# The last two blocks' down projection by two levels of a seven-product scheme instead of one

## Chip, cores and metric

The kernel runs on one core of a Trainium2 chip. The metric is the device time of one execution in microseconds (us). Times of the kernel before are the median of three runs; the profile is one further execution.

## The reference, cut to what matters

```python
kv  = np.einsum('bhsd,bhse->bhde', k, v)          # 8 batches, 8 heads, 576 positions, 64 wide
o   = np.einsum('bhsd,bhde->bhse', q, kv)
o   = o / np.sqrt(np.mean(o * o, -1, keepdims=True) + 1e-6) * g_norm
x   = o.transpose(0, 2, 1, 3).reshape(4608, 512)
g   = x @ w_gate                                  # 512 -> 1536
out = (g / (1 + np.exp(-g)) * (x @ w_val)) @ w_out   # 1536 -> 512, fp32
```

## The kernel before

The 4608 tokens are cut into nine blocks of 512 (0 to 8). Each block is taken through attention, then through the gate and value products ("up", 512 to 1536), then through w_out ("down", 1536 to 512). Matrix products are made by a scheme of seven block products for a 2 by 2 cut (a Strassen-like one, in the order 1, 5, 6, 2, 7, 4, 3 or a variant). Products 1, 6, 7, 4 accumulate one after another in one PSUM tile called b, 5 and 3 in one called c, and 2 in one called a; between two of them the partial sum is read out by ScalarE (copy) or VectorE (add). The scheme needs sums of blocks of both operands: side sums of h (the hidden activations), and differences of w_out's blocks.

Blocks 0, 1 and 2 go alone. From block 3 on, blocks go in pairs (class `Pair`): 3 and 4, 5 and 6, 7 and 8. In a pair's up stage both blocks are multiplied together and by two levels of the scheme, seven outer times seven inner products. For this, class `Inner` walks six pairs of feature columns, j = 0 to 5; each j has four groups of outer products, and each group makes its seven inner products. The weights' leaves for it lie in DRAM and stream through SBUF tiles `t` (nine buffers, class `Stream`, loads on SP's queue; a load is put in program order where the tile that it will replace is used for the last time). During group 2's products GpSimd makes four small additions (`made1`), after group 3 a 1024-wide one (`made2`), and after group 4 two 1024-wide multiplications (`made3`), which give h; then the side sums of block a's h. For j = 5 VectorE does the multiplications instead. All these results live in five ring buffers `r`.

The down stage (class `Down`, `multiply` in line 661's helper) is different: it takes one block after the other, and by one level. Each of a block's seven products is 12 matmuls: two output halves times six steps of 128 contracted features, 128 stationary columns and 256 moving ones. The moving operand is w_out (`wo`) or a difference of its quarters that GpSimd makes into `t` tiles (`turn_t`), so the results come out in rows of tokens and are stored as they are by SP's queue (`store`, line 1122). For the last block, the third product is made in two halves in PSUM tiles m (line 1032), the second of them as the very last work. The side sums of the second block of a pair (`second_sums`) are made by GpSimd during the first block's down stage. TensorE's order in a down stage is fixed as the program has it.

Line 816 is an inner product of the up stage, line 661 a product of the single-level stages, line 431 the attention's product with q, line 494 a transposition on TensorE. Lines 130, 131 and 132 are the helpers for additions, subtractions and multiplications; line 522 sends transposed pieces of x from SBUF to SBUF, 16 transfers of 64 KB on the queues of SP and ScalarE.

Of the kernel before, what the change touches and what calls it, by code (L numbers as in the profile page):

```python
# [8 lines left out]
F32 = mybir.dt.float32  # L9
# [9 lines left out]
def kernel(  # L19
# [84 lines left out]
    kvs = [consts.tile([P, NS, D], F32, name=f"kv{i}") for i in range(3)]  # L104
# [29 lines left out]
    @contextmanager  # L134
    def in_order(*engines):

        traced = nc.cur_bb.bb.instructions
        last = traced[-1]
        yield
        start = next(k for k in reversed(range(len(traced))) if traced[k] is last) + 1  # L140
        before = {}
        for i in traced[start:]:
            if engines and i.engine not in engines:
                continue
            if i.engine in before:
                tc.add_manual_dep(
                    i, before[i.engine].name,
                    mybir.DependencyInfo(mybir.DependencyClass.NoSync, mybir.DependencyReason.DATA), reason="order",
                )
            before[i.engine] = i  # L150

# [488 lines left out]
    class Quad:  # L640


        def __init__(self, steps):
            self.steps = steps
            self.ps, self.room = {}, None

            self.apart = {}

# [3 lines left out]
        def multiply(self, p):  # L652
            name, first = CHAIN[p]
            if first:
                tiles = [PSUMS[name].tile([P, 2, HB], F32, name=name) for _ in range(1 + (name in self.apart))]
                self.ps[name], self.apart[name] = tiles[0], tiles[-1]
            banks = self.ps[name], self.apart[name]
            for e, i in self.order(p):
                lhsT, rhs = self.operands(p, e, i)

                self.ffn.multiplied = nc.tensor.matmul(  # L661
                    banks[e][:, e], lhsT=lhsT, rhs=rhs, start=first and i == 0 and (e == 0 or banks[0] is not banks[1]),
                    stop=i == self.steps - 1, skip_group_check=True,
                )
            getattr(self, f"after{p}", lambda: None)()
# [91 lines left out]
    class Inner:  # L757
# [94 lines left out]
        def made3(self, p, e, q):  # L852
            if p != 4:
                return
            h = h_both[:, :, 2 * self.j : 2 * self.j + 2]
            halves = lambda t: t.rearrange("p (b e) t -> p b e t", b=2)
            c11, c12, c21, c22 = (self.whole(*i) for i in ((1, 1), (3, 1), (3, 0), (1, 0)))

            engine = nc.gpsimd if self.j + 1 < NP else nc.vector
            mul(engine, h[:, :, :, 0:HB], halves(c11), halves(c12))  # L860
            with tc.issue_after(self.ffn.fifth.ins):
                nc.scalar.activation(out=c21, in_=c21, func=ACT.Silu)
            mul(engine, h[:, :, :, HB:BLK], halves(c21), halves(c22))
            self.ffn.ended = self.ffn.a.h_sums(self.j, 1, engine)

# [13 lines left out]
    class Stream:  # L879
# [15 lines left out]
        def pump(self):  # L895

            while self.next and not self.held[-9]:
                n, j, c = key = self.next.pop(0)
                tile_ = t_tile(key)
                os, ps = JOINT[c]  # L900
                count = len(os) * len(ps)
                self.tiles[key] = tile_.rearrange("p a (b c) -> p (a b) c", c=P)
                self.uses[key] = count
                to = self.tiles[key][:, 0:count].rearrange("p (o i) c -> p o (i c)", o=len(os))
                src = self.dram[:, j, steps_of(OUTERS, os), steps_of(INNERS, ps)].rearrange("p o i c -> p o (i c)")
                nc.sync.dma_start(out=to, in_=src)

        def use(self, n, j, o, p):
            c, i = self.joint[o, p]
            key = n, j, c  # L910
            self.uses[key] -= 1
            if not self.uses[key]:
                self.free(key)
            return self.tiles[key][:, i]
# [4 lines left out]
    stream = Stream()  # L919
# [65 lines left out]
    class Down(Quad):  # L985
        def __init__(self, ffn):
            super().__init__(NP)
            self.ffn = ffn
            self.t = {}
            self.final = ffn.n == NB - 1  # L990
            self.lone = False
            self.opens = None
            self.keeps = False
            if self.final:
                self.apart["c"] = None
# [16 lines left out]
        def multiply(self, p, es=(0, 1)):  # L1012
            if p == 3 and self.lone:
                self.third(es)
                return
# [7 lines left out]
        def third(self, es):  # L1023


            if es[0] == 0:
                tiles = [m_psum.tile([P, 2, HB], F32, name="m") for _ in range(1 + self.final)]
                self.thirds = tiles[0], tiles[-1]
            for e in es:
                for i in range(self.steps):  # L1030
                    lhsT, rhs = self.operands(3, e, i)
                    self.ffn.multiplied = nc.tensor.matmul(  # L1032
                        self.thirds[e][:, e], lhsT=lhsT, rhs=rhs, start=i == 0 and (e == 0 or self.final),
                        stop=i == self.steps - 1, skip_group_check=True,
                    )
            if not self.final:
                add(nc.vector, self.o1[:, :, HD:DM], self.thirds[0], self.u2)
                self.ffn.store(self.o1, 0)
                return
            for e in es:  # L1040
                add(nc.vector, self.o1[:, e, HD:DM], self.thirds[e][:, e], self.u2[:, e])
                self.ffn.store(self.o1[:, e : e + 1, HD:DM], e, slice(HD, DM))

        def after6(self):
            super().after6()
            if self.lone:
                self.add_c(self.u2, self.u2)

        def order(self, p):
            order = [(e, i) for e in range(2) for i in range(self.steps)]  # L1050
            return order if p == 3 and self.final else sorted(order, key=lambda ei: ei[1])
# [17 lines left out]
        def rows(self):  # L1069
            o = ring()  # L1070
            self.o1, self.o2 = o[:, 0:2], o[:, 2:4]

        def after2(self):
            if self.lone:
                self.rows()
            add(nc.vector, self.o1[:, :, 0:HD], self.ps["a"], self.s)
            if self.final:
                self.ffn.store(self.o1[:, :, 0:HD], 0, slice(0, HD))
# [4 lines left out]
        def after7(self):  # L1083
            if not self.lone:
                self.rows()
            u3 = self.piece(2)
            nc.scalar.copy(out=u3, in_=self.ps["b"])
            self.add_c(self.o2[:, :, HD:DM], u3)
# [5 lines left out]
        def after3(self):  # L1094
            self.add_c(self.o1[:, :, HD:DM], self.u2)
            if not self.final:
                self.ffn.store(self.o1, 0)
                return
            for e in range(2):
                self.ffn.store(self.o1[:, e : e + 1, HD:DM], e, slice(HD, DM))  # L1100

        def add_c(self, o, u):

            if not self.final:
                add(nc.vector, o, self.ps["c"], u)
                return
            for e, c in enumerate((self.ps["c"], self.apart["c"])):
                add(nc.vector, o[:, e], c[:, e], u[:, e])

    class Ffn:  # L1110
# [9 lines left out]
        def store(self, o, t, columns=slice(None)):  # L1120
            rows = out[BLK * self.n : BLK * (self.n + 1), columns].rearrange("(t p) d -> p t d", t=T)
# [40 lines left out]
        def down(self, nxt, then={}):  # L1162
# [3 lines left out]
            down.lone = nxt is None  # L1166
            order = (1, 6, 5, 7, 2, 4, 3) if 5 in fill else (1, 5, 6, 7, 2, 4, 3)
            if down.lone:
                order = (1, 5, 6, 2, 7, 3, 4)
            for p in order:  # L1170
# [5 lines left out]
                with tc.issue_after(nxt.multiplied.ins) if self.n == 0 and p in (5, 6) else ExitStack():  # L1176
                    down.multiply(p, *[(0,)] * (p == 3 and down.lone and down.final))
# [14 lines left out]
            if down.lone and down.final:  # L1192
                down.multiply(3, (1,))
# [25 lines left out]
    class Pair:  # L1219


        def __init__(self, n):
            self.n = n
            self.a, self.b = (Ffn(i, blocks[i]) for i in (n, n + 1))
            self.visited = None

        def up(self, fill):

            a = self.a
            a.s1 = s_pool.tile([P, NP, HB], F32, name="s1")  # L1230
# [5 lines left out]
            for i, this in enumerate(units):  # L1236
                for unit, p in this.sequence(last):
                    if unit:
                        visited, self.visited = self.visited, None
                        with tc.issue_after(visited.ins) if visited else ExitStack():  # L1240
                            unit.multiply(p)
                last = this
                fill.get(i + 1, lambda: None)()
            a.down_ = Down(a)
            a.down_.keeps = True
            a.down_.turn_t(5)
# [3 lines left out]
            a.ended = self.ended  # L1250
# [165 lines left out]
    for n in range(PAIRED, NB, 2):  # L1416
# [3 lines left out]
        if after:  # L1420
# [10 lines left out]
            for i in range(8):  # L1431
                fill[12 + i] = lambda i=i, after=after: after[i // 4].load_quarters(i % 4 // 2, (i % 2,))
        pair.up(fill)
        if after:
            after[0].turn()
        if len(after) > 2:
            after[2].load_kv(0)
        with in_order(nc.tensor.engine):
            pair.a.down(after[0] if after else None, {5: pair.second_sums})
            if after:  # L1440
                after[1].turn()
            if len(after) > 2:
                after[2].load_kv(1)
            pair.b.down(after[1] if after else None)
# [31 lines left out]
```

## Time and profile before

| | |
|---|---|
| median of 3 runs | 1011.48 us (1011.41 to 1013.13) |
| profiled execution | 1012.7 us |
| its span, first to last instruction | 1010.9 us |
| TensorE busy | 993.7 us, 98% |
| VectorE, GpSimd, ScalarE busy | 673.7, 369.6, 232.2 us |
| granted TensorE clock | full (1.000) |
| up stage of blocks 7 and 8 | 806.1 to 934.85 us |
| down stage of block 7, then 8 | 934.85 to 1007.4 us |

PE in the profile is TensorE's matmul side, PEld its weight loads (which run beside the matmuls), DVE is VectorE, ACT is ScalarE, POOL is GpSimd and SP is SyncE, which here only issues DMAs. A line of a timeline has the start, the length, the engine, the line of the code, the operation, the tiles that it writes and reads, the shape and the count; what stands in brackets is the idle time before it and what ended it. An fp32 matmul of the code shows as two records. Every time after a start is counted in us from the first instruction.

### The profile page before, as it was taken

To read this page: it belongs to the slowest core of one execution; us is meant where nothing else is said; L and a number is where in the kernel's file an instruction comes from. 1 tells how busy PE (TensorE), PEld (TensorE's weight loads), DVE (VectorE), ACT (ScalarE), POOL (GpSimd) and SP (SyncE) were. 2 spreads that over 40 slices of the span, in tenths; PEclk is the share of its full clock that TensorE was granted. 3 is DMA by queue.
4 is the path that set the end of the run, shared out by engine and by line. 5 is a ranking of instruction groups with operands and counts; after the bars stand their busy time and mean duration, and the time that the engine had idled before them with its cause. 6 is when DMAs were issued, how large, how long until landed. Compare 5 with 4: busy or idle time off the path is not lost.

```text
span 1010.9 us, 17078 instructions
## 1 busy us (share of the span) xinstructions
PE 993.7 (98%) x6506; PEld 831.6 (82%) x6506; DVE 673.7 (67%) x1121; ACT 232.2 (23%) x367; POOL 369.6 (37%) x290
## 2 busy tenths in 40 slices
PE   5999999999999999999999999999999999999998
PEld 4544688888888888888888888888888888888887
DVE  2999797589868477656676746666668566666311
ACT  2665111221122311212211121121112121121000
POOL 0000263255544240445456004455660026546600
PEclk9999999999999999999999999999999999999999
DMA  8688653483866855767742464667221654553011
GB/s 220 198 266 260 120 93 136 97 288 97 210 136 122 214 114 158 189 179 182 170 130 42 111 164 135 182 164 191 77 42 43 146 164 144 150 145 101 1 42 42
DMA packets 254290, 143.23 MB, mean 142 GB/s; under 512 B 149504, under 2 KB 236544, under 8 KB 254208
## 3 DMA queue, kind: packets, MB, share of 16 engines
q1 hardware_dynamic: 223488, 138.20, 50.8%
q10 hardware_dynamic: 30656, 3.94, 2.5%
q8 instruction: 52, 0.85, 0.4%
q14 instruction: 30, 0.25, 0.1%
q0 software_dynamic: 64, 0.00, 0.0%
HBM read 104.99 MB, written 28.70 MB: 132 GB/s over the span
## 4 chain that ended last, share of the span: by engine, by line
PE 75%; DMA 1%; POOL 0%; SPq 0%; issue 0%; DVE 0%; POOLq 0%
PE b L816 22%; PE b L661 20%; PE c L816 11%; PE c L661 9%; PE a L816 5%; PE a L661 5%; PE m L431 1%; PE m L1032 1%; PE m L370 1%; DMA ld<-in_v_dram 1%; POOL t L131 0%; SPq L312 0%; PE b L370 0%; PE b L431 0%; PE a L431 0%
## 5 line engine op out<-in xcount | busy, mean ns | idle before, releaser
L816 PE MATMUL b<-arena,t 128*128 128x256 f32 x1008 | 244.5, 381 | 0.0
L816 PEld LDWEIGHTS b<-arena,t 128*128 128x128 f32 x1008 | 190.1, 190 | 29.6 <-DVE r L130 2.4
L130 POOL TENSOR_TENSOR r<-r 128x256 f32<-128x256 f32 (+1 forms) x90 | 94.7, 1054 | 246.1 <-DVE r L130 154.9
L130 DVE TENSOR_TENSOR r<-b,r 128x512 f32<-128x512 f32 (+1 forms) x234 | 138.9, 606 | 60.1 <-PE b L816 54.8
L130 DVE TENSOR_TENSOR r<-c,r 128x512 f32<-128x512 f32 (+1 forms) x170 | 104.5, 623 | 81.9 <-PE c L816 40.1
L132 POOL TENSOR_TENSOR arena<-r 128x1024 f32<-128x1024 f32 (+1 forms) x54 | 102.1, 1904 | 112.3 <-DVE r L130 67.9
L131 POOL TENSOR_TENSOR t<-wo 128x512 f32<-128x512 f32 x54 | 76.9, 1445 | 167.8 <-DVE wo L130 105.9
L130 DVE TENSOR_TENSOR r<-a,r 128x512 f32<-128x512 f32 x93 | 59.2, 636 | 108.3 <-PE a L661 70.7
L816 PE MATMUL c<-arena,t 128*128 128x256 f32 x504 | 122.5, 379 | 0.0
L131 DVE TENSOR_TENSOR arena<-arena 128x512 f32<-128x512 f32 (+3 forms) x96 | 104.3, 1101 | 20.0 <-PE b L661 17.7
L816 PEld LDWEIGHTS c<-arena,t 128*128 128x128 f32 x504 | 95.6, 190 | 13.5 <-issue 0.3
L661 PE MATMUL b<-wo,arena 128*128 128x256 f32 x432 | 98.1, 382 | 0.2
L661 PE MATMUL b<-t,arena 128*128 128x256 f32 x432 | 96.2, 379 | 0.0
L661 PEld LDWEIGHTS b<-wo,arena 128*128 128x128 f32 x432 | 81.2, 190 | 12.5 <-DVE arena L132 0.9
L661 PEld LDWEIGHTS b<-t,arena 128*128 128x128 f32 x432 | 82.1, 190 | 11.2
L830 ACT COPY r<-b 128x512 f32<-128x512 f32 x54 | 31.7, 586 | 189.9 <-PE b L816 189.9
L131 POOL TENSOR_TENSOR t<-arena 128x512 f32<-128x512 f32 x36 | 51.1, 1432 | 56.2 <-PE c L661 21.9
L816 PE MATMUL a<-arena,t 128*128 128x256 f32 x252 | 66.1, 379 | 0.0
L816 PEld LDWEIGHTS a<-arena,t 128*128 128x128 f32 x252 | 47.9, 190 | 6.5
L661 PE MATMUL c<-t,s 128*128 128x256 f32 x216 | 48.1, 379 | 0.0
L661 PE MATMUL a<-wo,arena 128*128 128x256 f32 x216 | 48.1, 379 | 0.0
L661 PEld LDWEIGHTS a<-wo,arena 128*128 128x128 f32 x216 | 41.0, 190 | 5.6
(115 smaller groups left out, 1242.9 us busy)
## 6 DMA issues: line engine op xcount, KB each, us to landing
t<-w SPq DMA_DIRECT2D x180, 256.0 KB, 3.1
out_dram<-r SPq DMA_DIRECT2D x17, 512.0 KB, 2.9
ld<-in_k_dram SPq DMA_DIRECT2D x26, 288.0 KB, 4.6
ld<-in_v_dram SPq DMA_DIRECT2D x26, 288.0 KB, 6.1
t<-w SPq DMA_DIRECT2D x54, 128.0 KB, 2.3
ld<-in_moe_w_gate_dram SPq DMA_DIRECT2D x12, 512.0 KB, 4.6
ld<-in_moe_w_val_dram SPq DMA_DIRECT2D x12, 512.0 KB, 4.7
ld<-in_moe_w_out_dram SPq DMA_DIRECT2D x12, 512.0 KB, 4.8
```

The costliest lines, as they stand in the source:

```text
L130: add = lambda e, o, a, b: e.tensor_tensor(out=o, in0=a, in1=b, op=OP.add)
L131: sub = lambda e, o, a, b: e.tensor_tensor(out=o, in0=a, in1=b, op=OP.subtract)
L132: mul = lambda e, o, a, b: e.tensor_tensor(out=o, in0=a, in1=b, op=OP.mult)
L370: self.positions = nc.tensor.matmul(self.kv_ps[r][u * D : (u + 1) * D, g, :], lhsT=k[:, u, c, :], rhs=v[:, u, c, :], start=(c == 0), stop= ...
L431: self.multiplied = nc.tensor.matmul(self.ps[i][u][p : p + D, t, j, :], lhsT=self.qt[rows, tile_t, head, p : p + D], rhs=kvs[b % 3][rows, ...
L661: self.ffn.multiplied = nc.tensor.matmul(banks[e][:, e], lhsT=lhsT, rhs=rhs, start=first and i == 0 and (e == 0 or banks[0] is not banks[1 ...
L816: self.ffn.multiplied = nc.tensor.matmul(ps[:, i], lhsT=stream.use(self.ffn.n, self.j, o, p), rhs=self.operand(o, p), start=first and i == ...
L830: copied = nc.scalar.copy(out=dst, in_=ps)
L1032: self.ffn.multiplied = nc.tensor.matmul(self.thirds[e][:, e], lhsT=lhsT, rhs=rhs, start=i == 0 and (e == 0 or self.final), stop=i == self ...
```

## The change

Blocks 7 and 8 no longer go through `Down`. Classes `Last` and `Deep` take both together and by two levels: seven outer products (grouped (1, 2), (6, 5), (7), (4, 3)) of seven inner ones of three contraction steps. Now w_out's block is the stationary operand and h the moving one: 128 tokens of each of the two blocks, 256 columns. So the results come out turned (features on partitions). Two of the four quarters of the output are transposed by VectorE in blocks of 32 by 32 and sent in 16 transfers of 32 KB each, with pieces of 128 bytes (`send`). The other two come from the last group: three of its four pieces are transposed back by TensorE (`turn_back`). The fourth is the last inner product (number 4 of the last group). Its addend is put into PSUM by four matmuls with the identity, and the product itself is made on top of it with h stationary and w_out moving, so in rows of tokens, as 12 matmuls of 128 columns (`turn_onto`).

The outer and inner side sums of h are made by VectorE in `down` (`outer`, `sum_x`). The weights' inner sums are made by GpSimd in the up stage of blocks 7 and 8: `prepare` lists them, and `tick`, called after every inner product, puts one at a time behind GpSimd's latest instruction at fixed places of a turn (`FIRST`, `TURNS`). First come six operations on wo in place, then nine times a leaf block (one 512-wide, one 128-wide and one 256-wide operation) whose results are written to DRAM by two transfers on SP's queue six ticks later, and twelve differences kept in SBUF. The side sums of h are now made for both blocks at once, 512 wide, twelve ticks after the multiplications, and for every second j four more operations turn them (`turn`). The leaves of outer products 5, 7 and 4 come back as 21 loads behind the last stream loads. The order of TensorE and VectorE in the new stage is that of the program. The kv tiles become one tile with three parts. Code that served only the last block's old form is dropped. Blocks 0 to 6 keep their code path.

```diff
+        def turned_block(self, i, c):
...
+            def send():
+                with behind(nc.sync.engine):
+                    nc.sync.dma_start(out=to[:, 0:5], in_=t)
+                    nc.sync.dma_start(out=to[:, 5:7], in_=more)
+
+            def differences():
+                sub(nc.gpsimd, t[:, 4], t[:, 0], t[:, 1])
+                sub(nc.gpsimd, more, t[:, 2:4], t[:, 1:2].to_broadcast([P, 2, P]))
+                self.sends.append((self.count + 6, send))
...
+        FIRST = {0: (0, 1, 3), 1: (0, 2, 4), 2: (1, 4), 3: (0, 2, 4, 5)}
+        TURNS = {0: (0, 1), 1: (), 2: (4,), 3: (0, 2, 4, 5)}
+
+        def tick(self):
+            g, e = divmod(self.count % 28, 7)
+            self.count += 1
+            if self.sends and self.sends[0][0] <= self.count:
+                self.sends.pop(0)[1]()
+            due = self.due and self.due[0][0] <= self.count
+            if due and (g, e) in ((2, 5), (2, 6)):
+                step = self.due.pop(0)[1]
+            elif e in (self.TURNS if self.count > 28 else self.FIRST)[g]:
+                step = self.due.pop(0)[1] if due else self.later.pop(0) if self.later else None
...
+        def turn_onto(self, last, between):
...
+            for i in range(2):
+                for f in range(2):
+                    nc.tensor.matmul(
+                        ps[:, i, f], lhsT=last.dst[:, i, f, e, q], rhs=ident,
+                        start=(i == 0 and f == 0), stop=False, skip_group_check=True,
+                    )
+            to = self.rows[:, e, q]
+            for i, o in enumerate(last.outers):
+                for f in range(2):
+                    for c in range(3):
+                        nc.tensor.matmul(
+                            ps[:, i, f], lhsT=self.operand(o, 4, c)[:, f], rhs=self.weight(o, 4, c),
+                            start=False, stop=c == 2, skip_group_check=True,
+                        )
+                if i == 0:
+                    between()
+            nc.scalar.copy(out=to[:, 0], in_=ps[:, 0])
+            nc.scalar.dma_start(out=self.rows_of(e, q, 0), in_=to[:, 0])
+            nc.vector.tensor_copy(out=to[:, 1], in_=ps[:, 1])
+            nc.sync.dma_start(out=self.rows_of(e, q, 1), in_=to[:, 1])
+
+        def down(self):
...
+            run(self.turn(2, 0))
+            m(0, 1, (0, 1))
+            m(0, 2, (0, 1))
+            m(0, 1, (2,))
+            self.sum_x(0, 1, 2)
+            m(0, 2, (2,))
+            m(0, 6)
+            self.sum_x(1, 1, 2)
+            m(0, 5)
+            self.sum_x(2, 1, 2)
+            self.second()
+            run(self.turn(2, 1))
+            m(0, 7)
+            self.outer(5, ((0, 0), (0, 1)))
+            m(0, 3)
+            m(1, 1)
...
+            m(2, 4)
+            nc.vector.transpose(out=room[:, 0], in_=c11)
+            self.send(room[:, 0], 0, 0, nc.scalar)
+            m(3, 6)
+            add(nc.vector, c22, u3, c22)
+            m(3, 5)
+            nc.vector.transpose(out=room[:, 1], in_=c22)
+            self.send(room[:, 1], 1, 1, nc.sync, nc.sync, nc.sync, nc.scalar)
+            m(3, 2)
+            m(3, 7)
+            self.hold(g[3])
+            self.rows = ring().rearrange("p (e q) (o f d) -> p e q o f d", e=2, o=2, f=2)
+            m(3, 3)
+            self.turn_back(0, 0)
+            self.turn_back(1, 1)
+            self.turn_onto(g[3], lambda: self.turn_back(1, 0))
...
+        if pair.deep:
+            stream.leaves(pair.deep)
+            pair.up(fill)
+            with in_order(nc.tensor.engine, nc.vector.engine):
+                pair.deep.down()
+            continue
```

In `down`, `m(g, p)` is inner product p of group g, counted from 0.

## Prediction

> **What bounds the kernel now.** I read the page's busy shares and forty slices first, then the chain of waits over the last 70 us, the busy time by stage, and the timelines of GpSimd and VectorE inside one turn of the paired stage.
>
> ```profile
> PE 993.7 (98%) x6506; PEld 831.6 (82%) x6506; DVE 673.7 (67%) x1121; ACT 232.2 (23%) x367; POOL 369.6 (37%) x290
> ...
> PE   5999999999999999999999999999999999999998
> ...
> DVE  2999797589868477656676746666668566666311
> ...
> POOL 0000263255544240445456004455660026546600
> ```
>
> TensorE is full from slice 2 to the end, at full clock. In the last slices VectorE falls to 3 and 1 tenths and GpSimd to nothing: the end of the kernel is TensorE alone. The chain says the same; its columns are start, length and what ran.
>
> ```profile
> 997.18 2.59 PE m L1032 x12
> 999.77 5.18 PE b L661 x24
> 1004.95 2.60 PE m L1032 x12
> 1007.55 0.02 issue
> 1007.58 0.42 DVE r L130
> ```
>
> A product of the down stage takes 5.18 us. It is 12 matmuls in the code and 24 records (each fp32 matmul leaves two), so a matmul with 256 moving columns costs 0.432 us. Fourteen such products run from 934.85 to 1007.37 us, 72.5 us with no gap. After them come a 0.42 us add and a store; the span ends at 1010.9, 2.9 us after the add. Next, the busy time in two stages: the up stage of blocks 7 and 8, and their down stage.
>
> ```profile
> 806.10:934.85 128.75, 128.75 (x596) 112.81 (x595) 86.25 (x146) 25.71 (x35) 65.79 (x53) 1.00 0.47 139
> 934.85:1007.50 72.65, 72.65 (x337) 63.66 (x335) 16.34 (x19) 5.75 (x9) 16.29 (x12) 1.00 0.07 26
> ```
>
> The columns are PE, PEld, DVE, ACT, POOL. Fewer matmuls shorten the kernel one for one, as long as the sums that replace them fit on VectorE (16 of 73 us used below) and GpSimd (66 of 129 us used above).
>
> **What the skill says.** "VectorE: DVE Perf Modes", in its section on the TRN2 errata, prices an fp32 two-input operation at (N+151)/0.96 ns: 957 ns for N = 768, a size that the old kernel never runs. Here N = 896 took 1.09 us, which the formula gives too. "SBUF — State Buffer", section "SBUF: two separate sides", says that a VectorE operation with two SBUF inputs and a GpSimd operation that reads SBUF exclude each other for a whole instruction. The trace agrees:
>
> ```profile
> 254.16 6.25 DVE L131 TENSOR_TENSOR arena<-arena 128x512 f32<-128x512 f32 x4
> ...
> 764.11 0.65 DVE L130 TENSOR_TENSOR arena<-arena 128x512 f32<-128x512 f32 x1
> ...
> 766.85 1.09 DVE L130 TENSOR_TENSOR arena<-arena 128x896 f32<-128x896 f32 x1
> 767.86 3.33 DVE L131 TENSOR_TENSOR arena<-arena 128x896 f32<-128x896 f32 x3
> ```
>
> The 512-wide form costs 1.56 us apiece in the first line, where GpSimd runs, and 0.65 us alone. "DMA: Bandwidth & Descriptors", section "Specifications", wants 512 bytes or more per piece for full rate; the new first sends write 128-byte pieces to HBM, which no row of this trace shows.
>
> **Part 1, TensorE.** Two levels make 49 products of three matmuls: 147 matmuls with both blocks' 128 columns each, 256 in all. The last product (6 of them) is made as 12 matmuls of 128 columns, after 4 of 128 that turn the addend, and 12 transposes bring three more pieces back. The transposes of line 494 price the 128-column form:
>
> ```profile
> 28.71 1.06 PE L494 MATMUL m<-ident,r 128*128 128x128 f32 x8 [0.27 <-DVE r L132]
> ```
>
> Eight records, the last 0.272 us long: (1.06 - 0.272)/7 = 0.113 us a record, 0.225 us a matmul. So 141 x 0.432 + 28 x 0.225 = 60.9 + 6.3 = 67.2 us against 72.5: **5.3 us saved**, if nothing waits.
>
> **Part 2, GpSimd in the up stage.** At 128 and 384 elements no row exists; the line through 0.73 us (256) and 1.27 us (512) gives estimates of 0.45 and 1.0. Added: 6 operations of 512 on wo (7.6 us; they wait for block 6's last product to have read wo, which is so when the stage starts), nine leaf blocks of 512 + 128 + 256 (22.1), 12 kept differences of 384 (12.0), side sums of both blocks (10 x 1.27 in place of 10 x 0.73: 5.4) and 8 turns of 512 (10.2); three operations on t go (3.8). That is +53.5 us, 119 of 128.75 us: 93% full. What counts is lateness at its deadlines. One turn of the old queue:
>
> ```profile
> 860.53 1.59 POOL L130 TENSOR_TENSOR r<-r 128x256 f32<-128x256 f32 x2 [0.50 <-DVE r L130]
> 863.12 0.72 POOL L130 TENSOR_TENSOR r<-r 128x256 f32<-128x256 f32 x1 [1.00 <-DVE r L130]
> 864.48 0.73 POOL L130 TENSOR_TENSOR r<-r 128x256 f32<-128x256 f32 x1 [0.64 <-DVE r L130]
> 868.74 2.35 POOL L130 TENSOR_TENSOR r<-r 128x1024 f32<-128x1024 f32 x1 [3.53 <-DVE r L130]
> ```
>
> The first small add is over at 861.25; VectorE's add that reads it starts at 865.42. So an add may come 4.2 us late. Between the last small add of a turn and the first of the next lie 16.5 us, and 7.0 of them go to the 1024-wide add and two multiplications. The new queue's heavy turns (after pairs 1 and 3) put seven operations of 512, one of 384 and 1.2 us of smaller ones there (11.1 us): 18.1 in all, 1.6 to 2.1 us late. The light turns (9.5 us) just fit and catch up. Lateness stays under 4.2, so TensorE waits for nothing: **cost 0**, covered by that slack. VectorE's adds of this stage read PSUM and one SBUF operand, so the exclusion doesn't apply. Bounds: 0 below; a gain is excluded, since TensorE has no gap to close. Above, see the rival.
>
> SP's queue takes 18 leaf writes (nine of 320 and 128 KB, 4.1 MB) and 21 loads of 192 KB. The writes wait for GpSimd's differences, up to 2.2 us by the same queue; t<-w loads queued behind them run nine tiles ahead, and 14 tiles last 21.2 us, so some 13 us cover it: 0. ScalarE is 20% busy here and loses nothing.
>
> **Part 3, VectorE in the down stage.** Independent operations follow each other 0.08 us faster than their length (766.85 to 767.86 for one of 1.09). New: 21 extra sums and 12 side sums of 768 at 0.88 (29.0 us); 13 PSUM adds of 512 at 0.61 and 11 of 256 at 0.34 (11.7); seven operations of 1024 at 1.14 (8.0); six of 512 from SBUF (3.9); a last copy. Some 53 us in 67: it fits on average, so I laid both engines' orders side by side, with 0.2 us from matmul to VectorE and 0.12 back. Alone, VectorE is never late by more than 0.04 us. But GpSimd's last 1024-wide add and two kept differences end some 3.3 us into the stage, and VectorE's multiplication and its two turn operations (two SBUF inputs each) alternate with them. The turn then ends near 5.85 us; the third product wants it at 5.18: 0.8 us of wait. VectorE, now behind, gives the side sum for outer product 5 at 17.3 us, wanted at 16.34: 1.1 us more. Afterwards it is in time. **Cost 1.9 us**; ends 0 (GpSimd done early) and 5 (each 768 costs 1.1 us).
>
> **Part 4, the tail.** The last evacuation is a 256-wide copy instead of a 256-wide add, 0.42 both. But eight stores of 128 KB leave in the last 5 us, four of them within the final 1.2 us. Two such stores of the old kernel landed 1.7 us after issue. At 0.6 us for the bytes of each (218 GB/s, an estimate between the 135 GB/s of the turned transfers at 751 to 755 us and the 367 GB/s at 33 to 35 us) four in a row from t = 68.5, counted from the start of the stage, land at 68.5 + 1.1 + 2.4 = 72.0, a lone one issued at 69.7 at 71.4: **0.6 us**, between 0 and 2. The first sends, 32 of 32 KB, leave over 9 us earlier. On ScalarE's queue 20 of them stand before its three copies:
>
> ```profile
> 749.52 7.21 ACTq L522 DMA_DIRECT2D arena<-r  x8
> ```
>
> That is 0.9 us each for twice the size; at half, 16 take 7 us from t = 53, and four more end near 62, before the first copy is wanted at 63.7. Cost 0; up to 4 us if 32 KB also take 0.9.
>
> **Sum.** -5.3 + 1.9 + 0.6 = -2.8 us. The profiled execution was 1012.7 us with a span of 1010.9 (1.8 around it); I expect a span near 1008.1 and 1009.9 for its like. The median of the runs, 1011.48, is 1.2 below that execution, so 1011.48 - 2.8 = **1008.7 us** is the forecast on the medians' scale.
>
> **Rivals.** *No wait at all*: GpSimd ends early or VectorE wins the port; -5.3 + 0.6 gives 1006.8. Chance 0.17. *VectorE bounds the down stage*: strided 768-wide operations at 1.1 us add 33 x 0.15 = 5.0 us of work, of which some 3.1, by the same side-by-side orders, reach TensorE: 1011.8. Against it, the 896 row has the same kind of access and meets its formula. Chance 0.18. *Stores*: ScalarE's sends block its copies, 1012.7. Chance 0.05. *GpSimd bounds the up stage*, the one that ends slower: at 1.2 times my durations its 119 us become 143, plus 3 of forced gaps, 17 more than the stage has; less 4.2 of slack TensorE waits 13 us, giving 1021.7. The gain is gone from about 1.11 times, and each tenth costs 12 us. For it: 93% occupation on estimated durations, and an SP queue waiting for it. Against: its operations took 1.27 and 2.36 us beside a busy VectorE in this same stage. Chance 0.09. The main case has 0.51, its own range 1007.2 to 1009.8.
>
> **The numbers.** Within 0.2% is about 2.0 us either way, what a measurement of this kernel can tell from no change. Faster needs under 1009.46: most of the main case (0.46), no wait (0.17), a third of the VectorE case (0.06): 0.69. Slower, above 1013.5, is the GpSimd case and a rest, 0.11. Same 0.20. The range runs from no wait with a nearly free tail, 1006.1, to the edge of the VectorE and store cases, 1012.8.
>
> **What would show it.** Right: down products of 2.59 us, the whole stage 68 to 70 us; two TensorE waits for VectorE in its first 17 us; no TensorE wait in the up stage; GpSimd over 90% busy there. Wrong: gaps before group-four products in the up stage, t<-w loads landing late, VectorE rows of 768 over 1.0 us, or over 3.5 us from last matmul to end.

## The result, and the profile after

The changed kernel takes 1007.68 us (median of 6 runs, 1006.64 to 1009.03) against 1012.16 us (6 runs): ratio 0.9953, 95% interval 0.9941 to 0.9966. That is faster by 0.47%, more than the 0.2% that the forecast took for the least that can be told from no change. The medians differ by 4.5 us. The profiled execution took 1007.82 us with a span of 1006.0, 4.9 us shorter than the span before. The forecast was 1008.7, so the measured median lies 1.0 us below it and inside its range, 1006.1 to 1012.8.

In the changed kernel the lines have moved: line 818 is the inner product of the up stage (816 before), line 894 an inner product of the new down stage, and lines 131, 132 and 133 are the helpers for additions, subtractions and multiplications (130 to 132 before).

Busy time by stage (columns: length of the stretch, PE, PEld, DVE, ACT, POOL, clock, DMA share, GB/s). First the up stage of blocks 7 and 8 in the kernel before, then, in a view of its own, the up stage and the down stage of the changed kernel:

```profile
807.59:934.85 127.26, 127.26 (x589) 111.49 (x588) 84.96 (x144) 25.71 (x35) 65.79 (x53) 1.00 0.47 140
```

```profile
808.03:935.29 127.26, 127.26 (x590) 111.47 (x589) 87.72 (x146) 25.71 (x35) 113.18 (x99) 1.00 0.60 183
935.29:1001.50 66.21, 66.14 (x327) 58.22 (x325) 55.23 (x71) 6.56 (x12) 3.51 (x3) 1.00 0.27 63
```

The up stage, counted from the first record of its own product (line 816 before, 818 after) to the first down product, takes 127.26 us in both kernels, though GpSimd is busy for 113.2 us of it instead of 65.8. (The start of 806.1 in the table ahead is 1.5 us too early: TensorE was still at block 6's last product.) The down stage needs 66.2 us of TensorE instead of 72.5. VectorE is busy for 55 of them instead of 16.

The start of the up stage moves by itself: it lay between 804.8 and 808.6 us over all executions shown here. So below I count a kernel's time in two pieces, the up stage and the rest, which goes from the first down product to the end of the span. For the kernel before these are 127.26 and 1010.9 - 934.85 = 76.05 us; after, 127.26 and 1006.0 - 935.29 = 70.71 us. **The change is worth 5.3 us** by these two executions. Their spans differ by 0.44 us less, because the changed kernel's reached the up stage that much later. The interval of the ratio, 3.4 to 6.0 us of gain, holds 5.3.

The end of the changed kernel in its timeline. Line 1101 is the transposes of `turn_back`, 1103 and 1105 the copies and stores of what they give, 1125 the matmuls with the identity, 1133 the last product, 1139 and 1141 the copies of its two halves, 1140 and 1142 their stores. SPq and ACTq are the queues on which SP and ScalarE issue DMAs:

```profile
996.57 1.04 PE L1101 MATMUL m<-ident,r 128*128 128x128 f32 x8
...
997.44 1.06 PE L1125 MATMUL a<-ident,r 128*128 128x128 f32 x8
998.34 1.50 PE L1133 MATMUL a<-t,arena 128*128 128x128 f32 x12
998.75 1.07 ACT L1103 COPY r<-m 128x512 f32<-128x512 f32 x2 [24.46 <-DMA out_dram<-r]
999.36 3.03 SPq L1105 DMA_DIRECT2D out_dram<-r  x6
999.67 0.60 PE L1101 MATMUL m<-ident,r 128*128 128x128 f32 x4
1000.11 1.50 PE L1133 MATMUL a<-ld,arena 128*128 128x128 f32 x12
1000.31 0.59 ACT L1103 COPY r<-m 128x512 f32<-128x512 f32 x1 [0.49 <-PE m L1101]
1001.65 0.37 ACT L1139 COPY r<-a 128x256 f32<-128x256 f32 x1 [0.75 <-PE a L1133]
1002.05 0.40 ACTq L1140 DMA_DIRECT2D out_dram<-r  x1
1002.06 0.42 DVE L1141 COPY r<-a 128x256 f32<-128x256 f32 x1 [4.60 <-ACT r L1139]
1002.51 0.42 SPq L1142 DMA_DIRECT2D out_dram<-r  x1
```

Three things are to be seen. Eight transposes on TensorE (two pieces of four) are eight records, but four matmuls with the identity are eight records as well: a transpose costs one record, a matmul two. ScalarE's first copy came at 998.75, although its transposes were over near 997.0; until then its queue was issuing the small sends. And after the last matmul (its twelve records of about 0.113 us are over at 1001.45) ScalarE's copy and VectorE's copy run one after the other, so the last store leaves no sooner than 1002.51, and the span ends 3.49 us after that. Before, the last add started 0.2 us after the last matmul, and the span ended 2.9 us after the store left.

The start of the down stage on VectorE; the stage starts at 935.29:

```profile
936.34 1.61 DVE L133 TENSOR_TENSOR arena<-r 128x1024 f32<-128x1024 f32 x1
938.05 1.30 DVE L131 TENSOR_TENSOR arena<-arena 128x512 f32<-128x512 f32 x1
939.39 0.69 DVE L132 TENSOR_TENSOR arena<-arena 128x512 f32<-128x512 f32 x1
940.11 1.83 DVE L131 TENSOR_TENSOR arena<-arena 128x768 f32<-128x768 f32 x2
```

The first two are longer than 1.22 and 0.69, the lengths that the same forms have once GpSimd is done, by 0.39 and 0.61 us. GpSimd's last additions of the up stage and its last operations of all are these:

```profile
926.25 2.86 POOL L131 TENSOR_TENSOR r<-r 128x256 f32<-128x256 f32 x4
...
933.55 2.35 POOL L131 TENSOR_TENSOR r<-r 128x1024 f32<-128x1024 f32 x1
935.86 2.94 POOL L132 TENSOR_TENSOR ld<-wo 128x384 f32<-128x384 f32 x2
```

### The profile page after: what moved, and what is told of

Its sections match the earlier page's. It is cut to its first block, busy times and chain, and to the rows that moved or that the text cites. A ratio compares the mean times of both kernels' runs of the same rounds, so it can differ in the third digit from the quotient of the medians.

```text
span 1006.0 us, 17267 instructions
## 1 busy us (share of the span) xinstructions
PE 988.2 (98%) x6496; PEld 826.6 (82%) x6496; DVE 715.2 (71%) x1173; ACT 233.4 (23%) x371; POOL 408.2 (41%) x328
## 4 chain that ended last, share of the span: by engine, by line
PE 73%; DVE 2%; DMA 1%; SPq 0%; POOL 0%; issue 0%; ACT 0%; DVEq 0%; POOLq 0%
PE b L818 22%; PE b L663 16%; PE c L818 11%; PE c L663 8%; PE a L818 5%; PE a L663 4%; PE b L894 3%; PE c L894 1%; PE m L436 1%; PE m L375 1%; PE a L894 1%; DMA ld<-in_v_dram 1%; DVE arena L131 1%; DVE arena L132 0%; DMA t<-w 0%; DVE arena L133 0%
## 5 line engine op out<-in xcount | busy, mean ns | idle before, releaser
L818 PE MATMUL b<-arena,t 128*128 128x256 f32 x1008 | 244.5, 381 | 0.2 <-DMA t<-w 0.2
L131 DVE TENSOR_TENSOR r<-b,r 128x512 f32<-128x512 f32 (+1 forms) x247 | 146.1, 603 | 63.7 <-PE b L818 55.1
L131 DVE TENSOR_TENSOR r<-a,r 128x512 f32<-128x512 f32 x95 | 60.4, 635 | 98.8 <-PE a L663 65.9
L132 POOL TENSOR_TENSOR t<-wo 128x512 f32<-128x512 f32 x45 | 64.1, 1447 | 163.5 <-DVE wo L131 105.2
L132 DVE TENSOR_TENSOR arena<-arena 128x512 f32<-128x512 f32 (+4 forms) x117 | 122.4, 1064 | 9.3 <-PE b L663 6.9
L663 PE MATMUL b<-wo,arena 128*128 128x256 f32 x336 | 76.8, 382 | 0.2
L663 PE MATMUL b<-t,arena 128*128 128x256 f32 x336 | 74.8, 379 | 0.0
L663 PEld LDWEIGHTS b<-wo,arena 128*128 128x128 f32 x336 | 62.9, 190 | 10.1 <-DVE arena L133 0.9
L663 PEld LDWEIGHTS b<-t,arena 128*128 128x128 f32 x336 | 63.8, 190 | 8.7
L663 PE MATMUL b<-arena 128*128 128x256 f32 x192 | 45.5, 380 | 0.0
L663 PE MATMUL b<-arena,t 128*128 128x256 f32 x192 | 45.4, 379 | 0.0
L1515 PE MATMUL b<-arena 128*128 128x512 f32 (+1 forms) x104 | 43.5, 561 | 0.5 <-ACT arena L500 0.5
```

The costliest lines, as they stand in the source:

```text
L131: add = lambda e, o, a, b: e.tensor_tensor(out=o, in0=a, in1=b, op=OP.add)
L132: sub = lambda e, o, a, b: e.tensor_tensor(out=o, in0=a, in1=b, op=OP.subtract)
L663: self.ffn.multiplied = nc.tensor.matmul(ps[:, e], lhsT=lhsT, rhs=rhs, start=first and i == 0 and e == 0, stop=i == self.steps - 1, skip_g ...
L818: self.ffn.multiplied = nc.tensor.matmul(ps[:, i], lhsT=stream.use(self.ffn.n, self.j, o, p), rhs=self.operand(o, p), start=first and i == ...
L1515: nc.tensor.matmul(t, lhsT=w[f // 2][:, i, P * (f % 2) : P * (f % 2 + 1)], rhs=x[:, i, of], start=(i == 0), stop=(i == NS - 1),)
```

## Experiments

Every kernel is the changed one with one edit, but for pool_twice (two) and best (four); a pair of lines that starts with - and + is the edit. In this table "up" and "rest" are the two pieces defined above, in us.

| kernel | first down product | up | rest | rest against the changed kernel |
|---|---|---|---|---|
| before | 934.85 | 127.26 | 76.05 | +5.34 |
| changed | 935.29 | 127.26 | 70.71 | |
| plain_last | 935.83 | 127.26 | 70.67 | -0.04 |
| two_banks | 933.49 | 127.26 | 70.51 | -0.20 |
| sends_even | 934.15 | 127.26 | 70.25 | -0.46 |
| best | 934.38 | 127.26 | 69.52 | -1.19 |
| pool_kept | 932.05 | 127.26 | 74.65 | +3.94 |
| pool_late | 932.75 | 127.26 | 74.85 | +4.14 |
| pool_twice | 944.70 | 136.17 | 75.40 | +4.69 |
| dve_more | 933.88 | 127.26 | 72.52 | +1.81 |

The spans in the expectations hold for an up stage that starts where the changed kernel's did; what is compared is the difference of the pieces. Spans are given to 0.1 us, so the last two columns are good to about 0.1 us. Each kernel's pieces come from one execution. How well they repeat can be seen where the code is the same: in the changed kernel, two_banks and sends_even the last matmul starts 66.05 to 66.07 us after the first down product, and in the five kernels that share the changed kernel's tail (changed, the three pool kernels, dve_more) 3.4 to 3.5 us pass from the start of the last store to the end.

### The second part of the change alone: plain_last

```diff
-            self.hold(g[3])
...
-            self.turn_onto(g[3], lambda: self.turn_back(1, 0))
+            m(3, 4)
+            self.turn_back(1, 0)
+            self.turn_back(0, 1)
```

> Undoes the second part of the change alone: the last inner product is made like the others (6 matmuls of 256 columns, VectorE's add, four transposes, ScalarE's copy of 512, two stores) instead of in rows of tokens onto its turned addend. By the trace of the changed kernel TensorE has 2.59 + 0.45 us of work in place of 4 x 0.225 + 12 x 0.225 = 3.6, but the last transposes wait 0.55 us for the add, and copy and two stores follow: span about 0.3 us longer than the changed kernel (1006.3), so nearly all of the gain is that of the two levels. Rival: making the last product in rows is what shortens the tail, and without it the span grows by 1 us or more (1007 or above).

Measured: 1007.38 us (5 runs), ratio to the kernel before 0.9948, 0.9934 to 0.9963, and a rest of 70.67 us. The 0.3 us that were expected to be lost did not show: the last store left 0.3 us later, counted from the first down product, and landed that much faster. So the rows of tokens bring nothing that can be seen, and the rival is refuted: the whole gain that can be seen belongs to the two levels.

### GpSimd's list lengthened: pool_kept and pool_twice

```diff
                         lambda o=o, b=b, x=x, k=k, n=n: [sub(
                             nc.gpsimd, self.kept[o][:, x], b[:, :, k, n], b[:, :, 0, 1]
-                        )
+                        ) for _ in range(2)]
```

> GpSimd makes each of its twelve kept differences twice (12 more operations of 384, 12 us, its list 1.10 times as long); results are the same. Theory: TensorE waits in the up stage only once the small additions come more than 4.2 us late; by the queue's order with the traced lengths they come 6.0 us late in the last turn, so TensorE waits some 2 us in the up stage, and 1 to 2 us more in the down stage, where GpSimd's last operations hold VectorE: span 1009 to 1010. Rival: GpSimd's occupation itself counts, and all 12 us are paid (1018).

Measured: up stage 127.26, so TensorE did not wait there at all; the rest 3.94 us longer. The sum is what was expected, the place is not, so that the sum fits is luck.

```profile
924.33 2.79 POOL L131 TENSOR_TENSOR r<-r 128x256 f32<-128x256 f32 x4
```

These are GpSimd's small additions of the last turn. They start 7.72 us before the first down product, where one that follows VectorE's add at once, as GpSimd's do in most turns, starts 10.8 before it: 3.1 us late, not 6.0. I had put 0.05 us between its operations, and the four above follow each other some 0.04 us faster than their lengths; that this is the whole difference is not shown. At 3.1 us late they stay within the slack of 4.2.

> As the one before, and the 512-wide difference of each of the nine leaf blocks twice too (23 us more, 1.2 times). Theory: the additions come 16.8 us late in the last turn, less 4.2 us of slack TensorE waits 12 to 13 us in the up stage and 1 to 2 more at the start of the down stage: span 1019 to 1021, slower than the kernel before. Rival: SP's queue, which waits for GpSimd before each leaf write, starves the stream of weight tiles, and TensorE waits for loads instead of additions.

Its edit is pool_kept's and the doubled 512-wide operation of each leaf block. Measured: span 1020.1 and 1021.91 us in all, slower than the kernel before. TensorE waits 8.9 us in the up stage, not 12 to 13, and the rest is 4.7 us longer, not 1 to 2: the sum fits again, the split does not. TensorE's waits in the up stage of this kernel, from the view of who waited for whom:

```profile
PEld b L818 <- DVE r L131: 7.4, 5, 2.1
...
PE b L818 <- DVE r L131: 5.5, 4, 1.7
...
PE c L818 <- DMA t<-w: 1.0, 2, 0.6
...
PEld b L818 <- DMA t<-w: 0.5, 1, 0.5
```

The columns are total, count and longest. PE and PEld can count the same gap, so the rows do not add up. Between TensorE's matmuls some 6.5 us lie at four products that wait for VectorE's adds, which wait for GpSimd's additions. Some 2 us lie at four others; the view puts three of those gaps, 1.5 us, down to a weight tile that came late. So the rival with SP's queue is there too, as the smaller part: in this kernel the queue waited for GpSimd before leaf writes, 8.3 us at the longest. In the last turn the additions, and the add of VectorE that waits for the first of them, stand here:

```profile
938.16 2.77 POOL L131 TENSOR_TENSOR r<-r 128x256 f32<-128x256 f32 x4
...
938.91 0.69 DVE L131 TENSOR_TENSOR r<-b,r 128x512 f32<-128x512 f32 x1 [2.54 <-POOL r L131]
```

The additions start 6.54 us before the first down product instead of 10.8, so after all of TensorE's waits they are still 4.3 us late: the slack of 4.2 us that the forecast read off the old trace is what the queue runs up against. The rival that ends slower therefore exists, with its threshold; the change stays below it.

### GpSimd at the start of the down stage: pool_late

```diff
-            self.later += kept
+            self.later += kept[:-2] + [lambda s=s: [s() for _ in range(4)] for s in kept[-2:]]
```

> Only GpSimd's very last two differences are made four times each (6 us more, all after its last 1024-wide addition). Theory: VectorE's operations with two SBUF inputs take turns with GpSimd's at the start of the down stage; eight of them there delay VectorE by 3 to 5 us, and TensorE waits 2.5 to 4 us for it in the first 17 us of the stage (0.3 in the changed kernel): span 1008.5 to 1010. Rival: the engines don't exclude each other, VectorE's lengths stay, and the span stays at 1006.

Measured: rest 4.14 us longer, a little more than the 2.5 to 4 expected. VectorE and GpSimd in this kernel (the stage starts at 932.75):

```profile
936.86 1.37 DVE L132 TENSOR_TENSOR arena<-arena 128x512 f32<-128x512 f32 x1
938.27 3.31 DVE L131 TENSOR_TENSOR arena<-arena 128x768 f32<-128x768 f32 x2
941.50 0.68 DVE L131 TENSOR_TENSOR r<-a,r 128x512 f32<-128x512 f32 x1
942.10 5.36 DVE L132 TENSOR_TENSOR arena<-arena 128x768 f32<-128x768 f32 x4
```

```profile
933.33 12.44 POOL L132 TENSOR_TENSOR ld<-wo 128x384 f32<-128x384 f32 x8
```

The two 768-wide operations at 938.27 take about 1.65 us each instead of 0.95, and GpSimd's 384-wide ones 1.55 on average instead of 1.0. The add at 941.50, whose one input is in PSUM, keeps its 0.68, as the add of the up stage at 938.91 in pool_twice keeps its 0.69 beside GpSimd's additions. Both engines lose, and only where VectorE has two SBUF inputs. This fits the exclusion that "SBUF — State Buffer" ("SBUF: two separate sides") describes, and an edit on GpSimd alone brought it about; the rival is refuted. By the page the operation that comes second waits for the whole of the first. The recorded lengths do not show that in full: one operation of each in turn would need 0.95 + 1.0 = 1.95 us a pair, and the pair takes about 1.6. Which part of the two overlaps is not shown.

It also says where pool_kept's 3.9 us went. There GpSimd's 1024-wide addition and its last four differences meet the same VectorE operations, and the addition takes 3.33 us instead of 2.35:

```profile
933.72 3.33 POOL L131 TENSOR_TENSOR r<-r 128x1024 f32<-128x1024 f32 x1
937.00 6.19 POOL L132 TENSOR_TENSOR ld<-wo 128x384 f32<-128x384 f32 x4
```

### VectorE's reserve: dve_more

```diff
             self.sum_x(2, 4)
+            for x in range(3):
+                self.sum_x(x, 4)
             m(2, 7)
```

> VectorE makes the three inner sums of outer product 4 twice (three more operations of 768, 2.6 us, in the middle of the down stage). Theory: VectorE's reserve there is 0.4 us by the trace (the add of the last group's first product ends 0.4 us before its second product starts), so TensorE waits about 1.9 to 2.2 us at that product: span 1007.9 to 1008.2. Rival: VectorE, 82% busy in the stage, catches up and nothing is lost.

Measured: rest 1.81 us longer for 2.6 us of work. The wait is where it was expected, one wait for an add that reads PSUM:

```profile
PEld b L894 <- DVE r L131: 2.1, 1, 2.1
```

(The wait of a weight load counts some 0.2 us that TensorE does not lose: between its matmuls the gap is 1.9 us.) The reserve at this place is 0.7 to 0.8 us instead of 0.4, and what goes beyond it is paid. VectorE at 83% of the stage (55.2 of 66.2 us) does not catch up, since the sums come in the order in which TensorE uses them.

### The tail: two_banks, sends_even, and a better kernel

two_banks gives the halves of the last product a PSUM tile each:

```diff
-            ps = a_psum.tile([P, 2, 2, P], F32, name="a")
+            pss = [a_psum.tile([P, 2, 2, P], F32, name="a"), c_psum.tile([P, 2, 2, P], F32, name="c")]
```

> The two halves of the last product lie in two PSUM tiles (a and c) instead of one. Theory: in the changed kernel ScalarE's copy of half 0 waited for the last matmul and VectorE's copy of half 1 for ScalarE, because both halves lie in one PSUM tile; with two tiles ScalarE's copy comes at once after its copy before, and VectorE's starts 0.4 us earlier. But SP's queue issues the last turned piece's two stores until then, so the last store leaves at most 0.1 us earlier: span 1005.9 to 1006.0. Rival: the copies' order sets the end, and the span shrinks by 0.4 us.

Measured: rest 0.20 us shorter, between the 0.1 at most of the theory and the 0.4 of the rival. The two copies did come apart:

```profile
998.08 0.37 ACT L1139 COPY r<-a 128x256 f32<-128x256 f32 x1
...
999.86 0.42 DVE L1141 COPY r<-c 128x256 f32<-128x256 f32 x1 [4.19 <-PE c L1133]
1000.84 0.42 SPq L1142 DMA_DIRECT2D out_dram<-r  x1
```

VectorE is done at 1000.28, and the store leaves at 1000.84, because SP's queue issues the last turned piece until 1000.72. So with the order of the copies out of the way the store leaves no earlier (67.35 us after the first down product, 67.22 in the changed kernel); SP's queue was next in line. What is shorter is the landing: 3.16 us from the last store to the end instead of 3.49. ScalarE's store of the other half had gone 2.3 us before it instead of 0.5, which may be why; that is not tested apart.

sends_even shares the 32 small sends out evenly:

```diff
-            self.send(room[:, 0], 0, 0, nc.scalar)
+            self.send(room[:, 0], 0, 0, nc.sync, nc.scalar)
...
-            self.send(room[:, 1], 1, 1, nc.sync, nc.sync, nc.sync, nc.scalar)
+            self.send(room[:, 1], 1, 1, nc.sync, nc.scalar)
```

> The 32 transfers of 32 KB alternate between SP's and ScalarE's queues (8 and 8 for each quarter) instead of 16 on ScalarE's, then 12 on SP's and 4 on ScalarE's. Theory: in the changed kernel ScalarE issued until 998.7, so its first copy of a turned piece started 1.5 us late, and SP's six stores of them were packed into the last 3 us; with even queues the first copy starts near 997.3 to 997.5, SP is free by 1001.9 and the last store, less crowded, lands in about 2.0 us instead of 2.4: span 0.2 to 0.5 us shorter. Rival: the copies were not on the path and the span stays at 1006.0 within 0.1.

Measured: rest 0.46 us shorter. ScalarE's first copy starts 0.7 us after the transposes begin instead of 2.2. The last store leaves no earlier (67.24 us after the first down product, 67.22 in the changed kernel), but only 3.01 us pass from it to the end. The stores ahead of it had left earlier, which fits the expectation that a less crowded store lands faster.

best puts both edits together, moves the last store to ScalarE's queue, and has GpSimd take two places more in the first turn (`FIRST[1] = (0, 1, 2, 3, 4)`).

> Two PSUM tiles for the last product, even queues for the sends, the last store on ScalarE's queue, and GpSimd's weight differences two places earlier in the first turn, so that it ends before the down stage. Theory: 0.4 us from the copies, 0.3 us from the stores, 0.3 us from the wait for VectorE at the start of the down stage: span near 1005.0, about 1 us below the changed kernel, and no wait of TensorE for VectorE in the down stage. Rival: the tail is set by the landing of the last store alone, and the span shrinks by 0.3 us or less.

Measured: 1004.83 us (4 runs), ratio to the kernel before 0.9921, 0.9906 to 0.9936; the rest is 69.52 us, 1.19 shorter than the changed kernel's. GpSimd now ends with the 1024-wide addition, early enough:

```profile
932.63 2.37 POOL L131 TENSOR_TENSOR r<-r 128x1024 f32<-128x1024 f32 x1
```

VectorE's first two operations have 1.23 and 0.69 us again, and TensorE's wait for the side sum of outer product 5 is gone: the last matmul starts 65.71 us after the first down product instead of 66.05. The end of this kernel:

```profile
998.86 1.50 PE L1133 MATMUL c<-ld,arena 128*128 128x128 f32 x12
...
1000.40 0.42 DVE L1141 COPY r<-c 128x256 f32<-128x256 f32 x1 [4.19 <-PE c L1133]
1000.86 0.40 ACTq L1142 DMA_DIRECT2D out_dram<-r  x1
```

The last store leaves 0.4 us sooner after the last matmul than in the changed kernel and lands 0.4 us faster; with the 0.34 us of TensorE these are the 1.19 us. This kernel beats both others by its pieces. The intervals of the two ratios to the kernel before do not overlap (0.9936 lies below the changed kernel's 0.9941), so the times agree on the order. The medians differ by 2.85 us, more than the 1.19 of the pieces; the start of the up stage, which moves by itself, can be the rest.

## Why the forecast was right, and which of its terms were off

| term of the sum | forecast | measured |
|---|---|---|
| TensorE's work in the down stage | -5.3 | -6.65 |
| waits in the up stage | 0 | 0 |
| waits for VectorE in the down stage | +1.9 | +0.3 |
| tail | +0.6 | +1.0 |
| sum | -2.8 | -5.34 |

*Part 1, TensorE.* The step that failed is the price of the 28 narrow matmuls. The forecast took "eight records" of line 494 for four matmuls and paid 0.225 us for each transpose. The code before has 16 transposes in that line and the trace 16 records: one each, 0.113 us. Twelve transposes at 0.113 and 16 matmuls at 0.225 make 4.95 us, and the trace has 4.88 from 996.57 to 1001.45. With 141 x 0.432 the stage holds 65.9 us of work, 72.5 - 65.9 = 6.65 less than before. The larger price, 0.432 us, was right.

*Part 2, GpSimd in the up stage.* Right: no wait, at 113 of 127 us. The mechanism is right too: in the changed kernel the small additions come 1.5 and 1.8 us late in the turns after the two heavy ones, where 1.6 to 2.1 was forecast, and on time in the others. The estimated lengths (0.45 and 1.0 us) were met by 0.46 and 1.00. pool_twice confirms the slack of 4.2 us as the limit. Under a longer list the additions were less late than reckoned, so even 12 us more on it brought no wait in that stage. The break-even that the forecast put at 1.11 times may still be near there: by the pieces a list 1.10 times as long keeps 1.4 us of the gain, and one 1.2 times as long is 8.3 us slower than the kernel before. But the first losses come at the start of the down stage, which that reckoning left out. The forecast's 13 us of cover for the weight tiles was not tested at the change's own list; in pool_twice some of them were late.

*Part 3, VectorE.* The mechanism is right (pool_late), its place too: the one wait is that for the side sum of outer product 5. The size was wrong. I let VectorE lose its turn to both kept differences before the third product; it lost 0.39 and 0.61 us and had the turn ready 4.8 us into the stage, not 5.85, before the product wanted it. So the 0.8 us wait did not come, and of the 1.1 us one 0.3 were left; best, where GpSimd ends early, has its last matmul 0.34 us sooner. The length of a 768-wide operation, 0.95 us, is the one that the formula in "VectorE: DVE Perf Modes" gives (957 ns), and the profile after shows it in every such line that GpSimd leaves alone.

*Part 4, the tail.* The crowding was seen, the chain was not. 0.6 us are the slower landing (3.49 instead of 2.86), which is the forecast's term. The other 0.4 are the last store leaving later: 1.06 us after the last matmul instead of 0.66. Two things hold it one behind the other, VectorE's copy waiting for ScalarE's and SP's queue issuing stores: two_banks takes away the first alone and the store leaves no earlier, best, among its four edits, takes away both, and it leaves 0.4 us sooner. ScalarE's sends took 11.9 us for 20, not about 9, and its copies came late, but TensorE did not wait for them.

*The rivals.* "No wait at all" described the waits best and still missed the sum, by the transposes' price. The store rival's mechanism exists and costs tenths, not 4 us. VectorE as the bound is near: dve_more shows that some 0.8 us more of work are free at its place, and no more.

*The signs.* Products of 2.59 us and an up stage without waits came as named. But the stage took 66.2 us, not 68 to 70, there was one wait in its first 17 us, not two, GpSimd was 89% busy, not over 90, and 4.5 us passed from the last matmul to the end, over the 3.5 that were named as a sign of being wrong.

Two of the wrong terms pulled one way (1.35 and 1.6 us) and the tail the other (0.4), so the change is 2.5 us larger than the sum said. That the median still came within 1.0 us is in part luck: the kernel before measured 1012.16 us over six runs, 0.7 more than the median of three that the forecast started from, and the medians differ by 4.5 us rather than 5.3. The main case's own range, 1007.2 to 1009.8, holds the measured time although most of its 1.9 us of waits did not come.

## What to carry to other kernels

A scheme that trades matmuls for sums is paid in TensorE time only if each sum is ready when its product starts: lay the engines' orders side by side and read the slack at each reader, since occupation (GpSimd 89%, VectorE 83% here) tells neither where the limit is nor where it breaks. Work that is free on GpSimd while VectorE reads PSUM is not free where VectorE reads two SBUF tensors, as pool_kept and pool_late show; end it before that stage begins. In a tail, look behind the wait that you remove: here a copy waited for a copy, and behind it the queue that issues the store was busy just as long.

## What the runs showed of the hardware

- An fp32 transpose on TensorE leaves one record of about 0.113 us, a matmul of the same 128 by 128 by 128 shape two (8 records for 8 transposes, and 8 for 4 matmuls with the identity).
- Where VectorE's operations have two SBUF inputs and GpSimd runs beside them, both slow down and neither is held for good: two 768-wide ones of VectorE took about 1.65 us each and GpSimd's 384-wide ones 1.55 on average, against 0.95 and 1.0 alone (pool_late).
- The 32 KB sends with pieces of 128 bytes to HBM landed 1.8 us (median, ScalarE's queue) and 2.0 us (SP's) after issue, no longer than the 128 KB stores with pieces of 512 bytes (2.0).
